# Attention outputs of two segments computed in the P @ V bank at the end of each unit, with six tiles of P

## The chip, the cores and the metric

The kernel runs on one core of one Trainium2 chip. The metric is the device time of one execution in microseconds (us). Before the change it is 1969.72 us, the median of 3 runs (1968.72 to 1974.34).

## The reference, cut to what matters

Two attentions over the same x (2048 rows, 512 columns, 32 heads of 16) are mixed by a gate per row. Side A is plain softmax attention over all 2048 keys. Side B works in four segments of 512 rows: causal attention inside the segment, plus a read from a linear memory that the segments before have filled.

```python
scores = jnp.einsum("bhqd,bhkd->bhqk", q, k) * scale      # A: all keys; B: own segment, masked
p = _softmax(scores, axis=-1)
o = jnp.einsum("bhqk,bhkd->bhqd", p, v)
a = o.reshape(B, S, D) @ wo
# B, per segment s:
o = g * (pq @ M) / (pq @ z + 1e-6) + (1.0 - g) * a_dot     # M, z: memory of the segments before
b = o @ wo
g = _sigmoid((x * gate_w).sum(-1, keepdims=True))
return g * a + (1 - g) * b
```

## The kernel before, in words

**Projections (the first 350 us or so).** q, k and v of both sides, the memory of side B and the gate are computed and left in DRAM.

**Units and slots.** The rest is attention. A unit is (side, group of 4 heads, segment of 512 query rows). Units of A and B alternate: A with 64 slots, then B with 10, so 74 slots a pair, 592 slots a segment (8 pairs) and 2368 in all, over four segments. A slot (`score_part`, L610) is one 512-column score product on TensorE into one of 3 `st` banks of PSUM; ScalarE turns it into P by an exponential (L633, and L630 for the last two slots of a B unit). Four slots fill one tile `p` of the pool `pp`, which has 4 such tiles.

**Maxima.** The scores of a unit need its row maxima first. For a unit that comes 96 slots later (`LEAD`), each slot also issues one product into one of 4 `sm` banks (`max_part`, L203), which VectorE reduces to a maximum (L218, L239, L243). The four banks are used in turn; `free` is the list of them.

**P @ V.** Slots come in bursts of three (`BURST`). After each burst `some_values` takes pieces of 128 columns of P from a queue, at most 3 (`MOST`), or 4 when the queue is longer than 8. Neighbouring pieces of one tile `p` go out as one group of four matmuls, one a head, side by side in four column strips of the array (L666). They add up in one PSUM bank, `ops`, for the whole unit. At the end of a unit ScalarE copies `ops` to SBUF (`oraw`, L670), and it goes to DRAM as `od`.

**Scaling.** `octet` handles 8 heads (two units) of a side, and also the memory read M. It has four steps at given slots: `load` (sums and values from DRAM, on SyncE's queue), `factors` 10 slots later (VectorE, L707 to L711), `factor` at 17 (the factors come back from DRAM, spread out, as `inv`), `scale` at 28 (GpSimd, L719, L721). For A and B it starts 16 slots after the end of the second unit's slots; the M octets start 14 slots apart, early in a segment.

**Outputs.** The scaled values times `wo` give the output: for a block of 128 rows, 8 octets by 4 column parts are 32 pieces (`piece`, L731), 128 a segment. `block_fill` borrows one of the four `sm` banks for a block, and the loop issues one piece after a burst, in a list `fill` that starts 24 slots after the segment's last A unit. So the outputs of segment 0 are made in the slots of segment 1, and so on; those of segment 3 partly at its end and partly after the loop. A burst in which a transposed maximum (L193) is due has no piece.

The order on TensorE is written out by this loop; its sequence in a burst is three times score and maximum product, then P @ V, then one piece or one transposed maximum.

```python
if n % BURST == BURST - 1 or n >= nS:
    some_values(n, MOST + (len(queue) > 8) if n < nS else 8)
```

Of the kernel before, what the change touches and what calls it, by code (L numbers as in the profile page):

```python
# [10 lines left out]
F32 = mybir.dt.float32  # L11
# [8 lines left out]
D = 512  # L20
H = 32
DH = 16
CH = 512
NCH = S // CH
KT = D // 128
NG = 8
NO = 4
# [8 lines left out]
LEAD = 96  # L36
BURST = 3
MOST = 3
GAP = {"A": 3, "B": 5}
MASK_T = 8  # L40
LATE_T = 8
# [5 lines left out]
def gated_mix(ctx, tc, x, xT, wqkv, a_wo, b_wq, b_wk, b_wv, b_wo, beta, gate_w, out):  # L47
# [508 lines left out]
    for (s, c), t in gate.items():  # L556
        nc.gpsimd.dma_start(t, gd["AB".index(s), c * CH:(c + 1) * CH].rearrange("(q t) -> q t", q=16)
                            .unsqueeze(0).broadcast_to([8, 16, 32]))
    pp = ctx.enter_context(tc.tile_pool(name="pp", bufs=4, reuse_waits="tile"))
    dp = ctx.enter_context(tc.tile_pool(name="dp", bufs=3, reuse_waits="tile"))  # L560
    va = ctx.enter_context(tc.tile_pool(name="va", bufs=2, reuse_waits="tile"))
    ob = ctx.enter_context(tc.tile_pool(name="ob", bufs=2, reuse_waits="tile"))
# [27 lines left out]
        vt[u] = t  # L590

    pt_ = {}
    stored = set()

    queue = []

    def score_part(n):

        u, j = slots[n]
        side, g, c = u  # L600
        q = qt[u]

        if j % 4 == 0:
            pt_[u, j // 4] = pp.tile([128, 4, CH], F32, tag="p", name="p")
        p = pt_[u, j // 4]
        h = (0, 2, 1, 3)[j % 4]

        def score(ps, h, b, k, n0, q0):

            nc.tensor.matmul(ps[:, n0:n0 + CH - q0], rows(k[:, :, b * 128:(b + 1) * 128], h, 50),  # L610
                             rows(q[:, :, q0:], h, 50), start=True, stop=True)

        def diagonal(x):
            nc.gpsimd.affine_select(out=x, in_=x, pattern=[[0, 4], [1, 128]], base=0, channel_multiplier=-1,  # L614
                                    compare_op=ALU.is_ge, fill=0.0)

        ps = st_ps.tile([128, CH], F32, tag="st", name="st")
        if side == "A":
            score(ps, h, j // 4 % 4, kt_[u, j // 16], 0, 0)
        else:  # L620
            k = kt_[u, c]
            if j < 8:
                score(ps, h, j // 4, k, 0, 128 * (j // 4))
                if j >= 4:
                    score(ps, h, 3, k, 384, 384)
            else:
                for f in range(2):
                    score(ps, 2 * (j - 8) + f, 2, k, 256 * f, 256)
        if side == "B" and j >= 8:
            nc.scalar.activation(p[:, 2 * (j - 8):2 * (j - 8) + 2, 0:256], ps.rearrange("p (h t) -> p h t", h=2), AF.Exp,  # L630
                                 scale=SCALE)
        else:
            nc.scalar.activation(p[:, h], ps, AF.Exp, scale=SCALE)  # L633
        if j % 4 == 3 or j == SLOTS[side] - 1:
            if side == "B":
                diagonal(p[:, :, 0:128])
                if j == 7:
                    diagonal(p[:, :, 384:])
            queue.extend((n + GAP[side], u, i) for i in range(j // 4 * 4, j + 1))

# [4 lines left out]
    def some_values(n, most):  # L645

        while queue and most and queue[0][0] <= n:
            _, u, i = queue.pop(0)
            most -= 1
            side, g, c = u  # L650
            w = 1
            while (queue and most and queue[0][0] <= n and queue[0][1] == u and (i + w) // 4 == i // 4
                   and (side == "A" or PIECES[i + w][0] == PIECES[i][0])):
                queue.pop(0)
                most -= 1
                w += 1
            p = pt_[u, i // 4]
            if side == "A":
                c0 = q0 = 128 * (i % 4)
                v = vt[u][:, i // 16, i // 4 % 4]  # L660
            else:
                b, c0, q0 = PIECES[i]
                v = vt[u][:, b]
            done = i + w == SLOTS[side]
            for h in range(4):
                nc.tensor.matmul(ops[32 * h:32 * h + 17, q0:q0 + 128 * w], v[:, 17 * h:17 * h + 17], p[:, h, c0:c0 + 128 * w],  # L666
                                 start=(i == 0), stop=done, tile_position=(0, 32 * h))
            if done:
                raw = ob.tile([128, CH], F32, tag="o", name="oraw")
                nc.scalar.copy(raw, ops)  # L670
                nc.sync.dma_start(od[side, c][4 * g:4 * g + 4].rearrange("h r t -> (h r) t"), raw)
                stored.add(u)
                return


# [3 lines left out]
        return rows.unsqueeze(0).broadcast_to([DH, 8, CH])  # L679

    held = {}


    beside = {}
# [4 lines left out]
    def octet(side, o, c, t0, vector=False):  # L689

        hs = slice(8 * o, 8 * o + 8)
        sums, rows, eng = (dend[c][hs], rdM[c][hs], nc.gpsimd) if side == "M" else (od[side, c][hs, 16], rd[side, c][hs], nc.gpsimd)
        if vector:
            eng = nc.vector
        k = {}

        def load():
            assert side == "M" or {(side, 2 * o, c), (side, 2 * o + 1, c)} <= stored
            k["rec"] = fr.tile([128, 32], F32, tag="rec", name="rec", bufs=3)
            nc.sync.dma_start(k["rec"], sums.rearrange("h (q t) -> h q t", q=16))  # L700
            if (side, c) not in held:
                held[side, c] = fr.tile([128, NO, CH], F32, tag="v" + side, name="v" + side, bufs=1 if side == "M" else 2)
            k["v"] = held[side, c][:, o]
            nc.sync.dma_start(k["v"], numd[c][:, o] if side == "M" else od[side, c][hs, 0:16].rearrange("h r t -> r h t"))

        def factors():
            nc.vector.reciprocal(k["rec"], k["rec"])  # L707
            if side == "B":
                nc.vector.scalar_tensor_tensor(k["rec"], k["rec"], ogh[:, o:o + 1], gate["B", c], op0=ALU.mult, op1=ALU.mult)
            else:  # L710
                nc.vector.tensor_mul(k["rec"], k["rec"], gate["A" if side == "A" else "B", c])  # L711
            nc.sync.dma_start(rows.rearrange("h (q t) -> (h q) t", q=16), k["rec"])

        def factor():
            k["inv"] = fr.tile([128, CH], F32, tag="inv", name="inv", bufs=4)
            nc.sync.dma_start(k["inv"], heads(rows))

        def scale():
            eng.tensor_mul(k["v"], k["v"], k["inv"])  # L719
            if side == "B" and c:  # L720
                eng.tensor_add(k["v"], k["v"], held["M", c][:, o])  # L721
        for n, f in ((0, load), (10, factors), (17, factor), (28, scale)):
            if t0 is None:
                f()
            else:
                at(t0 + n, f)

    def piece(ps, side, o, c, b, j, start, stop):

        for t in range(4):  # L730
            nc.tensor.matmul(ps[32 * t:32 * t + 32, 128 * j:128 * j + 128],  # L731
                             held[side, c][:, o, 128 * b + 32 * t:128 * b + 32 * t + 32], wos[side][:, o, 128 * j:128 * j + 128],
                             start=start, stop=stop, tile_position=(0, 32 * t))

# [6 lines left out]
    def block_fill(n, octets, c, b, then):  # L741

        ks = [(side, o) for o in octets for side in "AB"]
        for i in range(4 * len(ks)):
# [7 lines left out]
                    free.append(lent[c, b])  # L752
            fill.append((n, f))

    def leave(c, b):
        def then(ps):
            t = fr.tile([128, D], F32, tag="res", name="res", bufs=2)
            nc.scalar.copy(t, ps)
            nc.sync.dma_start(out_rows(c, b), t)
        return then  # L760
# [12 lines left out]
    at(180, lambda: load_wo("B", b_wo))  # L773
    last = NCH - 1
    for c in range(NCH):
        for o in range(NO):
            if c:

                octet("M", o, c, seg_end["B", c - 1] + (60 if c > 1 else 0) + 14 * o)
            for side in "AB":  # L780
                if (side, o, c) != ("A", NO - 1, last):
                    octet(side, o, c, end[side, 2 * o + 1, c] + 16)
        if c < last:
            for b in range(4):
                block_fill(seg_end["A", c] + 24, range(NO), c, b, leave(c, b))
    for b in range(4):
# [19 lines left out]
    while n < nS or queue or beside or filled[0] < len(fill):  # L806
# [12 lines left out]
            max_part(m, bank)  # L819
        run_todo(m)  # L820
        if n % BURST == BURST - 1 or n >= nS:
            some_values(n, MOST + (len(queue) > 8) if n < nS else 8)

            if any(e[0] < m + 1 for e in late):
                run_late(st_ps, "st", m + 1)
            else:
                for _ in range(1 if m < nS else 2):
                    if filled[0] < len(fill) and fill[filled[0]][0] <= n:
                        fill[filled[0]][1]()
                        filled[0] += 1  # L830
        n += 1
    octet("A", NO - 1, last, None, vector=True)
    for b in range(4):
        for j in range(4):
            close(0, "A", NO - 1, b, j)
            fill.pop()[1]()
        t = fr.tile([128, D], F32, tag="res", name="res", bufs=2)
        nc.vector.tensor_add(t, banks[b], part[b])
        (nc.scalar if b % 2 else nc.sync).dma_start(out_rows(last, b), t)
# [35 lines left out]
```

## Time and profile before

The profiled execution took 1971.88 us; its span is 1969.8 us, at a mean granted TensorE clock of 0.992. All times within the span count from its start.

| | |
|---|---|
| Median of 3 runs | 1969.72 us |
| Profiled execution, its span | 1971.88 us, 1969.8 us |
| TensorE (PE) busy | 98% |
| VectorE (DVE) busy | 82% |
| ScalarE (ACT) busy | 74% |
| DMA, mean | 116 GB/s |

The exponentials number the slots: by their starts, segment 0 begins at 348.1 us, segment 1 at 727.3, segment 2 at 1131.7, segment 3 at 1534.9, and the last slot is at 1944.2. PE rows are matmuls, PEld rows the loads of their weights. A float32 matmul of the program stands in the trace as two MATMULs, so one group of P @ V is x8, and one piece of an output is x8.

### The profile page before, as it was taken

The numbers are of one execution on the slowest core, as the hardware profiler recorded it, in microseconds if no ns is written. First come the engines' busy times: TensorE is split into PE (matmuls) and PEld (weight loads), VectorE is DVE, ScalarE is ACT, GpSimd is POOL, SyncE is SP. The second block draws the span as 40 slices with busy tenths as digits, with TensorE's granted clock in tenths as the row PEclk, the third lists the DMA queues.
The fourth block names the chain that finished last, engine by engine and source line by source line (L and its number), as shares of the span: only waits on it lengthen the run. The fifth ranks groups of instructions, "written<-read, shape, count | busy, mean of one in ns | idle before, by whom it ended". The sixth has DMA issues, their size and how long they took to land.

```text
span 1969.8 us, 50626 instructions
## 1 busy us (share of the span) xinstructions
PE 1932.7 (98%) x20361; PEld 1116.5 (57%) x20361; DVE 1618.2 (82%) x2768; ACT 1466.3 (74%) x2851; POOL 282.1 (14%) x497
## 2 busy tenths in 40 slices
PE   7999999999999999999999999999999999999997
PEld 5888765544444445555554455555544555555555
DVE  3235687899999998998999999999999999899820
ACT  3234332888888887888888887888888888888884
POOL 3000000211111112111112111111121112111210
PEclk9999999899999999999999999999999999999999
DMA  6567645334343435233324344324243343342211
GB/s 201 201 230 249 208 147 163 102 105 127 94 108 89 113 91 142 82 98 87 102 87 107 90 110 123 106 82 110 83 111 89 100 133 106 89 111 83 76 44 40
DMA packets 122504, 227.57 MB, mean 116 GB/s; under 512 B 34936, under 2 KB 46744, under 8 KB 121760
## 3 DMA queue, kind: packets, MB, share of 16 engines
q1 hardware_dynamic: 120688, 223.24, 38.9%
q8 instruction: 161, 2.64, 0.6%
q0 software_dynamic: 1296, 0.59, 0.2%
q14 instruction: 71, 0.58, 0.1%
q10 hardware_dynamic: 288, 0.52, 0.1%
HBM read 155.52 MB, written 67.52 MB: 113 GB/s over the span
## 4 chain that ended last, share of the span: by engine, by line
PE 91%; DVE 3%; DMA 2%; ACT 2%; issue 1%; SPq 0%; DVEq 0%; ACTq 0%
PE ops L666 30%; PE st L610 26%; PE sm L203 16%; PE pr L310 12%; PE sm L731 5%; DVE pm L218 2%; ACT p L633 1%; PE num L467 1%; PE mps L498 1%; PE mt_ps L193 1%; DMA qdA<-q 0%; ACT dg L229 0%; DMA raw<-xT 0%; DMA qdB<-q 0%; PE tps L490 0%
## 5 line engine op out<-in xcount | busy, mean ns | idle before, releaser
L633 ACT ACTIVATE p<-st 128x512 f32<-128x512 f32 x2304 | 1222.2, 605 | 239.7 <-PE sm L203 171.1
L218 DVE TENSOR_REDUCE pm<-sm 128x1 f32<-128x512 f32 x2048 | 1291.5, 683 | 117.3 <-PE sm L203 87.0
L203 PE MATMUL sm<-kA,qA 48*128 48x512 f32 x2048 | 786.4, 456 | 1.2 <-DVE pm L218 0.8
L610 PE MATMUL st<-qA,kA 50*128 50x512 f32 x2048 | 701.7, 438 | 3.8 <-ACT p L633 3.6
L666 PE MATMUL ops<-p,vA 128*17 128x384 f32 (+1 forms) x8184 | 576.5, 384 | 0.0
L610 PEld LDWEIGHTS st<-qA,kA 50*128 50x128 f32 x2048 | 332.8, 186 | 273.4 <-ACT p L633 203.3
L203 PEld LDWEIGHTS sm<-kA,qA 48*128 48x128 f32 x2048 | 338.6, 184 | 62.4 <-DVE pm L218 41.6
L666 PEld LDWEIGHTS ops<-p,vA 128*17 128x17 f32 x8184 | 165.0, 96 | 172.0 <-issue 161.7
L203 PE MATMUL sm<-kB,qB 48*128 48x128 f32 (+2 forms) x896 | 173.4, 297 | 0.4 <-DVE pmB L239 0.4
L203 PEld LDWEIGHTS sm<-kB,qB 48*128 48x128 f32 x896 | 134.4, 189 | 14.0 <-DVE pm L218 6.8
L230 POOL TENSOR_SCALAR_AFFINE_SELECT dg<-dg 128x512 f32<-128x512 f32 x128 | 81.2, 637 | 338.7 <-ACT dg L229 338.7
L610 PE MATMUL st<-qB,kB 50*128 50x384 f32 (+3 forms) x512 | 119.9, 341 | 2.7 <-ACT p L633 2.3
L358 DVE TENSOR_TENSOR q<-pr,q 128x512 fp32r<-128x512 f32 x64 | 44.0, 687 | 89.3 <-ACT q L351 79.6
L351 ACT CAST q<-pr 128x512 fp32r<-128x512 f32 x64 | 37.4, 585 | 98.5 <-PE pr L310 66.2
L731 PEld LDWEIGHTS sm<-woA,vA 128*32 128x32 f32 x2048 | 66.5, 113 | 69.1 <-issue 43.3
L731 PE MATMUL sm<-woA,vA 128*32 128x128 f32 x2048 | 98.0, 279 | 6.5 <-DVE vA L719 6.5
L610 PEld LDWEIGHTS st<-qB,kB 50*128 50x128 f32 x512 | 72.3, 185 | 50.7 <-ACT p L633 33.1
L731 PEld LDWEIGHTS sm<-woB,vB 128*32 128x32 f32 x2048 | 64.7, 110 | 63.1 <-issue 45.3
L186 POOL CAST ms<-nm 128x16 fp32r<-128x16 f32 x64 | 12.6, 197 | 599.4 <-DVE nm L179 540.2
L731 PE MATMUL sm<-woB,vB 128*32 128x128 f32 x2048 | 96.4, 273 | 0.0
L614 POOL TENSOR_SCALAR_AFFINE_SELECT p<-p 128x512 f32<-128x512 f32 x128 | 79.0, 635 | 100.2 <-ACT p L633 97.3
L666 PE MATMUL ops<-p,vB 128*17 128x128 f32 (+3 forms) x1104 | 89.6, 417 | 2.9 <-issue 2.3
(124 smaller groups left out, 1542.8 us busy)
## 6 DMA issues: line engine op xcount, KB each, us to landing
kA<-kdA SPq DMA_DIRECT2D x256, 128.0 KB
vA<-vdA SPq DMA_DIRECT2D x32, 544.0 KB
kA<-kdA SPq DMA_DIRECT2D x256, 64.0 KB
qdA<-q SPq DMA_DIRECT2D x32, 256.0 KB
kdA<-q SPq DMA_DIRECT2D x32, 256.0 KB
qdB<-q SPq DMA_DIRECT2D x32, 256.0 KB
qA<-qdA SPq DMA_DIRECT2D x64, 128.0 KB
kdB<-q SPq DMA_DIRECT2D x32, 256.0 KB
```

The costliest lines, as they stand in the source:

```text
L193: nc.tensor.matmul(pt[:32, :128], ms.rearrange("p r a h s -> p (r a h s)").bitcast(F32), identf, start=True, stop=True)
L203: nc.tensor.matmul(ps[:, n0:n0 + n], rows(qt[u][:, :, s * 128:(s + 1) * 128], h, 48), rows(k[:, :, k0:k0 + n], h, 48), start=True, stop=True)
L218: nc.vector.tensor_reduce(pm[:, h, s, kc:kc + 1], ps, axis=AX.X, op=ALU.max)
L230: nc.gpsimd.affine_select(out=dg, in_=dg, pattern=[[0, 4], [-1, 128]], base=0, channel_multiplier=1, compare_op=ALU.is_ge, fill=MASKED)
L310: nc.tensor.matmul(ps, l(a, k), r(b, k), start=(n == 0), stop=(n == 11))
L351: nc.scalar.copy(q1, ps)
L358: nc.vector.tensor_sub(q2, ps, q1.bitcast(F32))
L610: nc.tensor.matmul(ps[:, n0:n0 + CH - q0], rows(k[:, :, b * 128:(b + 1) * 128], h, 50), rows(q[:, :, q0:], h, 50), start=True, stop=True)
L614: nc.gpsimd.affine_select(out=x, in_=x, pattern=[[0, 4], [1, 128]], base=0, channel_multiplier=-1, compare_op=ALU.is_ge, fill=0.0)
L633: nc.scalar.activation(p[:, h], ps, AF.Exp, scale=SCALE)
L666: nc.tensor.matmul(ops[32 * h:32 * h + 17, q0:q0 + 128 * w], v[:, 17 * h:17 * h + 17], p[:, h, c0:c0 + 128 * w], start=(i == 0), stop=done ...
L731: nc.tensor.matmul(ps[32 * t:32 * t + 32, 128 * j:128 * j + 128], held[side, c][:, o, 128 * b + 32 * t:128 * b + 32 * t + 32], wos[side][: ...
```

## The change

- **P @ V falls behind.** The pool of P has 6 tiles in place of 4, and `some_values` takes a fourth piece when more than 6 pieces wait, in place of 8.
- **Outputs of segments 0 and 1** no longer go through `block_fill`. When an A unit of segment 1 or 2 has been stored, 16 pieces of the segment before are put on a list `shared`: one block of 128 rows, half of its columns. While the list has entries, each burst issues 4 of them in place of P @ V, in the bank `ops`, so for four bursts. Then ScalarE copies the half block (128 x 256) out and it is stored; two halves make a block.
- **Outputs of segments 2 and 3** are made as before, with a borrowed `sm` bank.
- **Octets** start when their two units have been stored: 8 slots later for A and B; an M octet starts 4 slots after the even B unit of its pair. The M values have two tiles of one octet in place of one of four, and `inv` has 3 tiles in place of 4.

```diff
+NP = 6
+SHARED = (0, 1)
...
-    pp = ctx.enter_context(tc.tile_pool(name="pp", bufs=4, reuse_waits="tile"))
+    pp = ctx.enter_context(tc.tile_pool(name="pp", bufs=NP, reuse_waits="tile"))
...
                 stored.add(u)
+                if side == "B" and c and g % 2 == 0:
+                    octet("M", g // 2, c, n + 4)
+                if (side, g ^ 1, c) in stored and u != ("A", NG - 1, NCH - 1):
+                    octet(side, g // 2, c, n + 8)
+                if side == "A" and c - 1 in SHARED:
+                    shared.extend(half_block(c - 1, g // 2, g % 2))
...
-            k["inv"] = fr.tile([128, CH], F32, tag="inv", name="inv", bufs=4)
+            k["inv"] = fr.tile([128, CH], F32, tag="inv", name="inv", bufs=3)
...
+    shared = []
+
+    def half_block(c, b, half):
+
+        ps = ops[:, 0:256]
+        ks = [(side, o) for o in range(NO) for side in "AB"]
+        for i in range(16):
+            def f(i=i):
+                piece(ps, *ks[i // 2], c, b, 2 * half + i % 2, i == 0, i == 15)
+                if i == 15:
+                    t = fr.tile([128, D], F32, tag="res", name="res", bufs=2)
+                    nc.scalar.copy(t[:, 0:256], ps)
+                    nc.sync.dma_start(out_rows(c, b)[:, 256 * half:256 * half + 256], t[:, 0:256])
+            yield f
...
-        for o in range(NO):
-            if c:
-
-                octet("M", o, c, seg_end["B", c - 1] + (60 if c > 1 else 0) + 14 * o)
-            for side in "AB":
-                if (side, o, c) != ("A", NO - 1, last):
-                    octet(side, o, c, end[side, 2 * o + 1, c] + 16)
-        if c < last:
+        if c < last and c not in SHARED:
             for b in range(4):
                 block_fill(seg_end["A", c] + 24, range(NO), c, b, leave(c, b))
...
         if n % BURST == BURST - 1 or n >= nS:
-            some_values(n, MOST + (len(queue) > 8) if n < nS else 8)
+            if shared:
+                for _ in range(4):
+                    shared.pop(0)()
+            else:
+                some_values(n, MOST + (len(queue) > 6) if n < nS else 8)
```

More of the change, by code (lines that the diff above doesn't have):

```diff
@@ L592, in gated_mix @@
     pt_ = {}
+    order_p = {}
     stored = set()
@@ L604, in score_part @@
             pt_[u, j // 4] = pp.tile([128, 4, CH], F32, tag="p", name="p")
+            order_p[u, j // 4] = len(order_p)
+            assert not queue or order_p[queue[0][1], queue[0][2] // 4] > len(order_p) - 1 - NP
         p = pt_[u, j // 4]
@@ L681, in gated_mix @@
     held = {}
+    scaled = set()
     beside = {}
@@ L700, in load @@
             nc.sync.dma_start(k["rec"], sums.rearrange("h (q t) -> h q t", q=16))
-            if (side, c) not in held:
-                held[side, c] = fr.tile([128, NO, CH], F32, tag="v" + side, name="v" + side, bufs=1 if side == "M" else 2)
-            k["v"] = held[side, c][:, o]
+            if side == "M":
+                k["v"] = held["M", c, o] = fr.tile([128, CH], F32, tag="vM", name="vM", bufs=2)
+            else:
+                if (side, c) not in held:
+                    held[side, c] = fr.tile([128, NO, CH], F32, tag="v" + side, name="v" + side, bufs=2)
+                k["v"] = held[side, c][:, o]
             nc.sync.dma_start(k["v"], numd[c][:, o] if side == "M" else od[side, c][hs, 0:16].rearrange("h r t -> r h t"))
@@ L720, in scale @@
             if side == "B" and c:
-                eng.tensor_add(k["v"], k["v"], held["M", c][:, o])
+                eng.tensor_add(k["v"], k["v"], held.pop(("M", c, o)))
+            scaled.add((side, o, c))
         for n, f in ((0, load), (10, factors), (17, factor), (28, scale)):
@@ L728, in piece @@
     def piece(ps, side, o, c, b, j, start, stop):
+        assert (side, o, c) in scaled
         for t in range(4):
-            nc.tensor.matmul(ps[32 * t:32 * t + 32, 128 * j:128 * j + 128],
+            nc.tensor.matmul(ps[32 * t:32 * t + 32, 128 * (j % (ps.shape[1] // 128)):128 * (j % (ps.shape[1] // 128)) + 128],
                              held[side, c][:, o, 128 * b + 32 * t:128 * b + 32 * t + 32], wos[side][:, o, 128 * j:128 * j + 128],
@@ L821, in gated_mix @@
         if n % BURST == BURST - 1 or n >= nS:
-            some_values(n, MOST + (len(queue) > 8) if n < nS else 8)
+            if shared:
+                for _ in range(4):
+                    shared.pop(0)()
+            else:
+                some_values(n, MOST + (len(queue) > 6) if n < nS else 8)
             if any(e[0] < m + 1 for e in late):
@@ L832, in gated_mix @@
     octet("A", NO - 1, last, None, vector=True)
+    assert len(stored) == len(units)
     for b in range(4):
```

## The prediction

> **What bounds the kernel now.** I read the busy shares first, then the stages, then the waits of two stages, then single bursts.
>
> The page's first part, and what the chain of waits says by line:
>
> ```profile
> span 1969.8 us, 50626 instructions
> ...
> PE 1932.7 (98%) x20361; PEld 1116.5 (57%) x20361; DVE 1618.2 (82%) x2768; ACT 1466.3 (74%) x2851; POOL 282.1 (14%) x497
> ...
> PE ops L666 30%; PE st L610 26%; PE sm L203 16%; PE pr L310 12%; PE sm L731 5%; DVE pm L218 2%; ACT p L633 1%; PE num L467 1%; PE mps L498 1%; PE mt_ps L193 1%; DMA qdA<-q 0%; ACT dg L229 0%; DMA raw<-xT 0%; DMA qdB<-q 0%; PE tps L490 0%
> ```
>
> TensorE looks like the bound, and nearly all of the chain lies on it. By stages it is less simple. Columns: stretch, us, then busy us of PE, PEld, DVE, ACT, POOL. The first three rows are six pairs of units without output pieces (segment 0), five pairs with them, and two stretches that are the whole of segments 1 and 2; the row after them is of L731 alone in the five pairs.
>
> ```profile
> 445.50:727.30 281.80, 278.43 (x2802) 137.88 (x2800) 273.44 (x469) 249.06 (x493) 42.36 (x79) 1.00 0.37 102
> ...
> 780.70:1037.50 256.80, 255.70 (x3210) 144.94 (x3208) 232.92 (x388) 211.35 (x415) 36.79 (x67) 1.00 0.33 93
> ```
>
> ```profile
> 727.30:1131.70 404.40, 402.10 (x4760) 220.11 (x4758) 372.75 (x633) 336.02 (x662) 65.94 (x112) 1.00 0.37 100
> 1131.70:1534.90 403.20, 400.82 (x4766) 219.79 (x4764) 373.09 (x633) 336.73 (x661) 66.81 (x112) 1.00 0.36 101
> ```
>
> ```profile
> 780.70:1037.50 256.80, 44.16 (x880) 28.39 (x880) 1.00 0.33 93
> ```
>
> A pair without pieces takes 281.8 / 6 = 47.0 us, or 1.90 us for each of its 24.67 bursts; there DVE is busy 273.44 / 281.8 = 97%. A pair with pieces takes 256.8 / 5 = 51.4 us, with 880 / 8 / 5 = 22 pieces, and DVE falls to 91%. So PE's busy share of 99% in both does not tell who waits; the waits do. Columns: us in total, times, longest. First 445.50 to 727.30, then 780.70 to 1037.50:
>
> ```profile
> PEld st L610 <- ACT p L633: 78.5, 175, 0.7
> ```
>
> ```profile
> PEld st L610 <- ACT p L633: 19.7, 88, 0.6
> ...
> DVE pm L218 <- PE sm L203: 16.2, 43, 1.0
> ```
>
> Without pieces PE waits for the banks that ScalarE and VectorE empty; with pieces VectorE waits for PE. Segments 1 and 2 pass from the one to the other: pieces in some 5 of 8 pairs, none in the rest.
>
> **The price of each kind of work on PE.** Rows are start and length; the difference between starts is what a step costs. In order: two pieces of P (after them a score), four pieces in two groups, a piece of an output behind four pieces in two groups, behind four in one group, and two pieces of an output.
>
> ```profile
> 560.00 0.63 PE L666 MATMUL ops<-p,vA 128*17 128x256 f32 x8
> 560.55 0.50 PE L610 MATMUL st<-qA,kA 50*128 50x512 f32 x1
> ...
> 561.80 0.52 PE L666 MATMUL ops<-p,vA 128*17 128x384 f32 x4
> ```
>
> ```profile
> 447.06 1.06 PE L666 MATMUL ops<-p,vB 128*17 128x384 f32 x16
> 448.05 0.49 PE L610 MATMUL st<-qA,kA 50*128 50x512 f32 x1
> ...
> 448.94 0.41 PE L666 MATMUL ops<-p,vB 128*17 128x256 f32 x4
> ```
>
> ```profile
> 719.61 1.06 PE L666 MATMUL ops<-p,vA 128*17 128x128 f32 x16
> 720.60 0.50 PE L610 MATMUL st<-qB,kB 50*128 50x512 f32 x1
> ...
> 721.58 0.30 PE L666 MATMUL ops<-p,vA 128*17 128x128 f32 x4
> ```
>
> ```profile
> 1004.85 1.06 PE L666 MATMUL ops<-p,vA 128*17 128x128 f32 x16
> 1005.73 0.40 PE L731 MATMUL sm<-woB,vB 128*32 128x128 f32 x8
> 1006.06 0.50 PE L610 MATMUL st<-qA,kA 50*128 50x512 f32 x1
> ```
>
> ```profile
> 831.09 1.05 PE L666 MATMUL ops<-p,vB 128*17 128x512 f32 x8
> 831.96 0.40 PE L731 MATMUL sm<-woA,vA 128*32 128x128 f32 x8
> ```
>
> ```profile
> 1896.14 0.62 PE L731 MATMUL sm<-woB,vB 128*32 128x128 f32 x16
> 1896.69 0.50 PE L610 MATMUL st<-qB,kB 50*128 50x512 f32 x2
> ```
>
> - Two pieces of P and the return to the scores: 0.55 us. Four: 0.99. So a piece is 0.22 and the return some 0.12.
> - An output piece and the return: 0.33; two: 0.55. So a piece of either kind costs 0.22, and the return is paid once a burst.
> - Four pieces of P in two groups: 0.88; in one group: 0.87. **Merging groups saves 0.01 us**, not a matmul's time.
> - Three exponentials in a row take 1.57 us and three maxima 1.88 (below).
> - Scores and maxima after four pieces: 0.89 (first) and 0.98 (last of the 40 such bursts of the first stretch); their mean is 0.96. After two pieces, 1.25: the short rest of the burst is given back, as ScalarE and VectorE are not done.
>
> ```profile
> 563.10 1.57 ACT L633 ACTIVATE p<-st 128x512 f32<-128x512 f32 x3 [0.43 <-PE sm L203]
> ...
> 564.22 1.88 DVE L218 TENSOR_REDUCE pm<-sm 128x1 f32<-128x512 f32 x3
> ```
>
> **The change, part by part.**
>
> *Merged groups.* In the order in which the two programs issue, groups of P @ V fall from 1161 to 742. 419 times 0.01 us is about 4 us over the kernel, within the sums below. The Trainium skill, "TensorE: Matmul & The Clock Gate", Part 1, gives a fixed cost of about 2.5 ns to each matmul; with 8 matmuls of the trace to a group that would be an estimated 8 us, and the rows show half of it.
>
> *Outputs moved.* The pieces of segments 0 and 1 stay 256, at 0.22 each wherever they stand: moving them saves no time of PE. What changes is the company they keep. In the changed order, segment 1 has 197 bursts: 127 with four pieces of P, 30 with four output pieces, 40 with one to three pieces of P. No bank is lent, so maxima have four. The sum for the segment:
> - 127 x (0.99 + 0.95) = 246. I take 0.95 and not 0.96, because in a row of long bursts ScalarE and VectorE have more time than in the 40 measured ones, which stand among short ones. Bounds: 0.89 and 1.05.
> - 30 x (0.33 + 3 x 0.22 + 1.15) = 64. These bursts fall on the slots of the B unit, whose scores come in several products. Such a burst is no cheaper than the one at 488.55 below, 1.16, and no dearer than that at 583.63, 1.50; I take the lower, as those after it have four pieces of rest.
> - 40 x 1.90 = 76, a short burst lasting what the stretch without pieces gives per burst.
> - 11 transposed maxima beside four pieces at some 0.2 us: 2 (two matmuls and a change; a guess between 0.1 and 0.3).
>
> ```profile
> 488.55 0.44 PE L610 MATMUL st<-qB,kB 50*128 50x384 f32 x1
> ...
> 489.71 0.30 PE L666 MATMUL ops<-p,vA 128*17 128x128 f32 x4
> ```
>
> ```profile
> 583.63 0.44 PE L610 MATMUL st<-qB,kB 50*128 50x384 f32 x1
> ...
> 585.13 0.52 PE L666 MATMUL ops<-p,vB 128*17 128x384 f32 x4 [0.47 <-issue]
> ```
>
> Together 388 us. From VectorE's side: its 372.75 us of work at the 97% that it reaches when it is the bound make 384. I take 387 for each of segments 1 and 2: 404.4 - 387 = 17.4 and 403.2 - 387 = 16.2, **33.6 us saved**. Ends: 373 (VectorE without a gap) and 404 (nothing gained).
>
> *Uneven P @ V in segments 0 and 3.* There the pieces of P per burst go from 3, 4, 3, 2 to 3, 1, 4, 4. In segment 0 VectorE is the bound at 97% and has a backlog of up to four banks at 0.63 us each, more than the 0.99 us of four pieces: nothing lost, 0. In segment 3 a bank is lent and an output piece stands in each burst, so two bursts in a row are long and starve VectorE, and the one-piece burst cannot give it all back: 0.08 us for each of some 49 cycles, **4 us lost**. Bounds for both: -3 and +21 (below).
>
> *The bank `ops`, handed over twice a unit.* A wait is added: P @ V of the next unit stands behind ScalarE's copy of the half block, and behind it on PE all scores. Before, P @ V waited 1.2 us in all for 64 such copies (the copy's view; "who waited for it"):
>
> ```profile
> L670 ACT COPY oraw<-ops x64: 586/608/632, 397.8 to 1946.6; 128x512 f32<-128x512 f32 x64
> ...
>   PEld ops L666: 1.2, 6
> ```
>
> A burst's scores and maxima lie between the hand-overs as before, and the new copy is half as wide. I take 0. Upper end: three exponentials ahead of the copy (1.57 us) and the copy at 0.6, less 0.95 of scores, 1.2 us; 32 hand-overs make 38 us. The Trainium skill, "PSUM — Partial Sum Buffer", section "PSUM bank collisions raise a hardware error", asks that two engines be kept apart by whole bank and quadrant; it speaks against putting a second user into this bank, since the unused half does not help, and the row above is what the trace shows of the price so far.
>
> *The rest at nothing.* Loads of octets move to 8 slots (some 5 us) after the store. The store and the load that waits for it on SyncE's queue took 1.99 and 2.06 us at the end of the kernel; k tiles queued behind are asked for 20 slots ahead. Without that cover, SyncE would hold them 2 to 4 us a unit. VectorE's factors keep their 10 slots after the load. Eight more stores, four full copies less and 16 half copies more change ScalarE's 83% by under 1%.
>
> ```profile
> 1947.19 1.99 DMA odA<-oraw
> ...
> 1949.19 2.06 DMA rec<-odA
> ```
>
> More tiles of P remove no wait that the rows show.
>
> **Sum.** 1971.88 (the profiled execution: span 1969.8 and 2.1 around it) - 33.6 + 4 = 1942.3. The median of the runs lies 2.2 lower, so 1940.
>
> **The rivals.**
> - *VectorE becomes the only bound in segments 1 and 2.* With four banks and long bursts it never starves: 375 us a segment, 57.6 saved, nothing lost in segment 3: 1912. For it: it reaches 97% today. Against: B-unit bursts stretch PE to 1.15 and more, and no backlog covers four in a row.
> - *Nothing is gained.* PE's work is unchanged but for 4 us; if the scores keep their present mean length behind any rest, segments 1 and 2 lose only that: 1966 to 1970. For it: PE shows 99% in every stage. Against: 0.96 after four pieces, 1.25 after two.
> - *Slower: uneven bursts.* A burst with one piece gives nothing back if its scores last 1.6 us or more (they wait for VectorE's banks and for exponentials), while the four-piece bursts still cost 1.95. A cycle of four then costs 0.2 us more; 98 cycles in segments 0 and 3 make 21 lost. The same starving at the end of the catch-up runs (scores 1.05, 0.1 more in each of 127 bursts) leaves segments 1 and 2 only 7 us: +7 on balance, 1977. For it: 1.25 already after two pieces. Against: VectorE at 97% in segment 0 cannot be held up by PE alone.
> - *Hand-overs at their upper end*: 38 us back, 1978; counted with the one before.
>
> **How the numbers follow.** A difference of 0.3% (6 us) is about what a measurement of this kernel can tell from none. Chances: forecast (1925 to 1955) 0.54; VectorE the only bound 0.18; a small gain, 1955 to 1964, 0.06; nothing gained 0.10; slower 0.12. Faster 0.78, same 0.10, slower 0.12. For eight in ten the range takes in the VectorE rival from 1914 up and most of the case of no gain: 1914 to 1968.
>
> **What would show it.** Right: segments 1 and 2 at 380 to 394 us with DVE at 95 to 98%, scores waiting for ScalarE less in them, groups x8 of 512 columns at 0.87 up to the next step, segment 0 within 3 us of before, segment 3 a few us longer. Wrong: P @ V or output pieces waiting for copies of `ops` for more than 5 us in all; VectorE waiting for PE over 20 us in a segment; a kA load that PE waits for.

## The result, and the profile after

The changed kernel takes 1940.28 us (median of 4 runs, 1939.61 to 1941.45), against 1969.82 us before (median of 4 runs, 1968.72 to 1974.34). The ratio is 0.9846, with a 95% interval of 0.9829 to 0.9863: faster by 29.5 us, where 29.7 were forecast.

The page of the changed kernel, first part and chain by line (L671 is P @ V, L615 the scores, L205 the products for the maxima, L748 the output pieces):

```profile
span 1938.8 us, 44063 instructions
...
PE 1897.4 (98%) x17009; PEld 993.5 (51%) x17009; DVE 1611.9 (83%) x2768; ACT 1467.0 (76%) x2859; POOL 281.7 (15%) x497
...
PE ops L671 30%; PE st L615 27%; PE sm L205 14%; PE pr L312 11%; PE ops L748 3%; PE sm L748 2%; ACT p L638 2%; DVE pm L220 1%; DMA qdA<-q 1%; PE num L469 1%; DMA kdB<-q 1%; PE mt_ps L195 1%; ACT dg L231 1%; PE mps L500 0%; DMA qdB<-q 0%
```

TensorE has 3352 MATMULs less in the trace and is as busy as before, 98%. The gain must be looked for by stages: stretch, us, then busy us of PE, PEld, DVE, ACT, POOL. The rows are six pairs of segment 0, the whole of segments 1 and 2, and the first seven pairs of segment 3.

```profile
444.10:728.10 284.00, 279.21 (x2240) 122.02 (x2240) 273.66 (x469) 248.52 (x493) 42.38 (x79) 0.99 0.37 101
728.10:1110.80 382.70, 380.49 (x3758) 177.88 (x3762) 368.71 (x633) 336.22 (x665) 65.50 (x112) 1.00 0.41 105
1110.80:1494.20 383.40, 380.67 (x3839) 178.35 (x3828) 369.55 (x634) 337.36 (x666) 67.06 (x114) 1.00 0.41 106
1494.20:1862.80 368.60, 365.29 (x3909) 188.81 (x3909) 316.27 (x534) 297.75 (x583) 60.14 (x102) 1.00 0.35 94
```

Segments 1 and 2 fell from 404.4 and 403.2 to 382.7 and 383.4, and VectorE works 96% of segment 1 in place of 92%. Segment 0 is 2 us longer, and segment 3 longer by far more than the forecast: to the last slot 419.7 us, against 409.3.

The waits between TensorE and VectorE in segment 1, before and after. Columns: us in total, times, longest.

```profile
PEld st L610 <- ACT p L633: 50.5, 162, 0.7
...
DVE pm L218 <- PE sm L203: 21.3, 53, 1.2
...
PEld sm L203 <- DVE pm L218: 11.8, 45, 0.6
```

```profile
PEld st L615 <- ACT p L638: 117.2, 184, 0.9
...
DVE pm L220 <- PE sm L205: 9.1, 20, 1.0
...
PEld sm L205 <- DVE pm L220: 1.1, 6, 0.2
```

Two waits shrank: VectorE's for a product, and TensorE's for a free `sm` bank (the weight load of a maximum product that waits for a reduction). The second, 11.8 us, has almost gone. The wait of score weights for ScalarE grew from 50.5 to 117.2 us, and the segment is shorter all the same: the total of this wait does not say how much time is lost by it.

### The profile page after: what moved, and what is told of

Its sections match the earlier page's. It is cut to its first block, busy times and chain, and to the rows that moved or that the text cites. A ratio compares the mean times of both kernels' runs of the same rounds, so it can differ in the third digit from the quotient of the medians.

```text
span 1938.8 us, 44063 instructions
## 1 busy us (share of the span) xinstructions
PE 1897.4 (98%) x17009; PEld 993.5 (51%) x17009; DVE 1611.9 (83%) x2768; ACT 1467.0 (76%) x2859; POOL 281.7 (15%) x497
## 4 chain that ended last, share of the span: by engine, by line
PE 89%; DMA 3%; ACT 3%; DVE 3%; issue 1%; POOL 0%; SPq 0%; ACTq 0%; POOLq 0%; DVEq 0%
PE ops L671 30%; PE st L615 27%; PE sm L205 14%; PE pr L312 11%; PE ops L748 3%; PE sm L748 2%; ACT p L638 2%; DVE pm L220 1%; DMA qdA<-q 1%; PE num L469 1%; DMA kdB<-q 1%; PE mt_ps L195 1%; ACT dg L231 1%; PE mps L500 0%; DMA qdB<-q 0%
## 5 line engine op out<-in xcount | busy, mean ns | idle before, releaser
L205 PE MATMUL sm<-kA,qA 48*128 48x512 f32 x2048 | 757.7, 450 | 1.3 <-DVE pm L220 1.3
L615 PE MATMUL st<-qA,kA 50*128 50x512 f32 x2048 | 702.9, 439 | 7.8 <-ACT p L638 7.1
L671 PE MATMUL ops<-p,vA 128*17 128x512 f32 (+2 forms) x4912 | 561.2, 529 | 0.0
L615 PEld LDWEIGHTS st<-qA,kA 50*128 50x128 f32 x2048 | 336.1, 186 | 412.6 <-ACT p L638 336.9
L205 PEld LDWEIGHTS sm<-kA,qA 48*128 48x128 f32 x2048 | 338.3, 185 | 37.7 <-DVE pm L220 22.9
L205 PE MATMUL sm<-kB,qB 48*128 48x128 f32 (+2 forms) x896 | 171.5, 295 | 0.6 <-DVE pmB L241 0.5
L671 PEld LDWEIGHTS ops<-p,vA 128*17 128x17 f32 x4912 | 81.7, 95 | 165.0 <-issue 153.9
L205 PEld LDWEIGHTS sm<-kB,qB 48*128 48x128 f32 x896 | 135.0, 188 | 10.6 <-DVE pm L220 2.6
L615 PE MATMUL st<-qB,kB 50*128 50x384 f32 (+3 forms) x512 | 120.9, 342 | 3.3 <-ACT p L638 2.4
L615 PEld LDWEIGHTS st<-qB,kB 50*128 50x128 f32 x512 | 72.6, 186 | 66.3 <-ACT p L638 52.0
L671 PE MATMUL ops<-p,vB 128*17 128x512 f32 (+3 forms) x1024 | 89.2, 444 | 1.7 <-issue 1.5
L241 DVE TENSOR_REDUCE pmB<-sm 128x4 f32<-128x512 f32 x128 | 87.1, 681 | 1.2 <-PE sm L205 1.2
L235 DVE TENSOR_REDUCE pmB<-dg 128x4 f32<-128x512 f32 x128 | 86.7, 677 | 0.8 <-POOL dg L232 0.8
L231 ACT COPY dg<-sm 128x512 f32<-128x512 f32 x128 | 76.4, 597 | 1.8 <-DVE pmB L235 1.8
L722 DVE RECIPROCAL rec<-rec 128x32 f32<-128x32 f32 x44 | 15.1, 343 | 71.2 <-DMA rec<-odA 40.3
```

The source lines that it names most:

```text
L205: nc.tensor.matmul(ps[:, n0:n0 + n], rows(qt[u][:, :, s * 128:(s + 1) * 128], h, 48), rows(k[:, :, k0:k0 + n], h, 48), start=True, stop=True)
L231: nc.scalar.copy(dg, blocked(ps))
L235: todo.append((m + MASK_T, lambda: nc.vector.tensor_reduce(to, dg.rearrange("p (h s) t -> p h s t", h=2), axis=AX.X, op=ALU.max)))
L241: nc.vector.tensor_reduce(pm[:, 1, h, 3:7], blocked(ps), axis=AX.X, op=ALU.max)
```

## The experiments

All segment times below are from the starts of the exponentials in one profiled execution of each kernel; medians are of 4 runs. A pair is an A and a B unit, 74 slots, eight to a segment. Segment 3 counts to the last slot.

| kernel | median | ratio (95%) | seg. 0 | seg. 1 | seg. 2 | seg. 3 |
|---|---|---|---|---|---|---|
| before | 1969.82 | | 379.2 | 404.4 | 403.2 | 409.3 |
| changed | 1940.28 | 0.9846 (0.9829 to 0.9863) | 381.4 | 382.7 | 383.4 | 419.7 |
| e1_no_shared | 1994.81 | 1.0124 (1.0107 to 1.0141) | 383.0 | 408.5 | 411.1 | 417.4 |
| e2_spread | 1983.09 | 1.0062 (1.0047 to 1.0077) | 379.6 | 409.7 | 408.9 | 410.9 |
| e3_three_banks | 1990.29 | 1.0094 (1.0079 to 1.0109) | 383.8 | 406.0 | 407.3 | 421.9 |
| e4_threshold | 1935.12 | 0.9813 (0.9796 to 0.9830) | 380.1 | 382.8 | 383.3 | 411.7 |
| e5_shared3 | 1919.68 | 0.9732 (0.9707 to 0.9757) | 385.3 | 382.7 | 383.3 | 396.5 |
| e6_both | 1917.90 | 0.9720 (0.9700 to 0.9740) | 382.9 | 382.7 | 383.3 | 396.5 |
| e7_bank_seg0 | 1990.75 | 1.0096 (1.0065 to 1.0127) | 400.2 | 404.7 | 403.3 | 409.2 |
| e8_four_banks | 1945.84 | 0.9854 (0.9825 to 0.9884) | 379.3 | 390.9 | 389.5 | 410.9 |
| e9_four_banks_spread | 1942.11 | 0.9852 (0.9838 to 0.9867) | 382.8 | 389.4 | 389.0 | 408.1 |
| e10_no_part | 1911.12 | 0.9697 (0.9681 to 0.9714) | 380.9 | 382.8 | 383.4 | 388.9 |

Segment 0's first pair alone varies from 50 to 55 us: it took 51.1 us before and 54.7 in e9_four_banks_spread, whose segment 0 is the same work. So 4 us in segment 0 mean little.

My theory at first was that of the prediction: segments 1 and 2 gain because output pieces are moved out of short stretches and into long bursts, in which scores and maxima do not wait; segments 0 and 3 lose by the uneven 3, 1, 4, 4. The rivals were the fourth `sm` bank, which is no longer lent, and the fewer groups of P @ V.

**No outputs at unit ends.**

```diff
-SHARED = (0, 1)
+SHARED = ()
```

> The changed kernel with all outputs made piece by piece in borrowed sm banks again; six tiles of P, the earlier fourth piece and the earlier octets stay. My theory: the merged groups are worth about 4 us of TensorE and the uneven 3, 1, 4, 4 costs more than that; what segment 3 lost in the changed kernel (10.4 us) is lost in segments 1 and 2 as well, so 1998 to 2008 us, slower than before. Rival, that fewer matmul groups and more tiles of P make the gain: 1940 to 1966 us. If the earlier octets cost or gain something, segment 1's first pair (53.4 us before, 47.8 after) shows it.

1994.8 us. The merged groups and six tiles of P make no gain; with the lent bank and without the output pieces at unit ends, segments 1 to 3 lose 4 to 8 us each. The first pair of segment 1 took 52.2 us, 1.2 less than before, and that of segment 2 took 53.2, 2.8 more: the earlier octets show no gain. The theory holds here in kind, 3 us below its range.

**The pieces spread out, in a lent bank.**

```diff
-                for _ in range(1 if m < nS else 2):
+                for _ in range(0 if 592 <= n < 1776 and n // BURST % 4 == 3 else 1 if m < nS else 2):
```

> The kernel before, with the output pieces of segments 0 and 1 left out of every fourth burst and so spread over the whole of the next segment (17 a pair in place of 22), still one a burst in a borrowed sm bank, P @ V as before. My theory, that gain comes from spreading the pieces over stretches where TensorE waits and from putting them into long bursts: the first half alone, segments 1 and 2 at 392 to 400 us, 1946 to 1962 us in all. Rival, that the gain is the fourth sm bank: nothing, 1966 to 1973 us.

Neither: 1983.1 us, slower than before. The bank is now lent through the whole of segments 1 and 2, and both are longer, 409.7 and 408.9. In segment 1 the seven later pairs hold 912 / 8 / 7 = 16 pieces each and take 357.1 / 7 = 51.0 us, hardly less than the pairs of before with 22 (51.4). The piece rows of those seven pairs:

```profile
779.60:1136.70 357.10, 45.76 (x912) 29.44 (x912) 1.00 0.32 92
```

Spreading pieces saves nothing if the bank stays away for longer. My theory fell here.

**The changed kernel with three banks.**

```diff
+        if n == 592:
+            kept = free.pop(0)
+        if n == 1776:
+            free.append(kept)
```

> The changed kernel with one sm bank laid aside during segments 1 and 2, so that maxima have three as when a block borrows one. My theory: 2 to 6 us more in each of the two segments, 1944 to 1952 us. Rival, that the gain is the fourth bank: both segments back at about 404 us, 1976 to 1984 us.

1990.3 us, above both ranges. My theory's 2 to 6 us a segment are far off. Segments 1 and 2 are back at 406 and 407 us, 2 to 4 us over the rival's 404, and segments 0 and 3 stay as long as in the changed kernel: without the fourth bank, everything else that the change does in segments 1 and 2 is worth nothing. The waits of this run in segment 1:

```profile
PEld sm L205 <- DVE pm L220: 17.2, 47, 0.7
DVE pm L220 <- PE sm L205: 16.4, 47, 1.0
```

TensorE's wait for a bank is 17.2 us, where the changed kernel has 1.1 and the kernel before 11.8; VectorE's wait for a product is 16.4, where they have 9.1 and 21.3. I read it so: three banks hold the products of one burst, so TensorE waits when VectorE is behind, and VectorE runs dry when TensorE then does four pieces of P.

**A lent bank without pieces.** The new theory needed the bank by itself. In the kernel before, segment 0 has no pieces; there a bank was laid aside.

```diff
+        if n == 0:
+            kept = free.pop(0)
+        if n == 592:
+            free.append(kept)
```

> The kernel before, with one sm bank laid aside during the slots of segment 0, where no output piece is issued; nothing else. New theory, after the spread pieces and the three banks: the lent bank itself makes a pair of units last 51 us, whether 16, 17 or 22 pieces are in it, so segment 0 goes from 379 to some 400 to 412 us without a single piece, 1990 to 2004 us in all. Rival, my first account, that a piece costs its 0.22 us of TensorE and the stretch with pieces is long for that: segment 0 longer by 0 to 6 us, 1970 to 1976 us.

Segment 0 takes 400.2 us in place of 379.2, without one instruction more in the program. Six pairs, with their waits:

```profile
451.40:747.70 296.30, 294.92 (x2801) 150.27 (x2800) 277.96 (x469) 251.18 (x493) 42.52 (x79) 1.00 0.35 97
```

```profile
PEld sm L203 <- DVE pm L218: 15.6, 56, 0.7
DVE pm L218 <- PE sm L203: 9.1, 23, 1.0
```

A pair goes from 47.0 to 49.4 us, 2.4 us for the bank alone, and the wait for a free bank rises from 4.2 to 15.6 us (the row of before is below). That is less than the 51 that I expected: the bank is not all of it.

```profile
DVE pm L218 <- PE sm L203: 6.1, 14, 1.0
...
PEld sm L203 <- DVE pm L218: 4.2, 19, 0.4
```

**Pieces without a lent bank.** The reverse: the kernel before, its pieces at their places, but added into `ops`.

```diff
...
+                if c < 2:
+                    piece(ops, *ks[i // 4], c, b, i % 4, None, None)
+                    if i == 4 * len(ks) - 1:
+                        then(wos["A"][:, 0])
+                    return
...
```

> The kernel before, with the pieces of segments 0 and 1 added into the bank of P @ V, at 17 columns of weights in place of 32, one a burst while a unit's sum is open, so that no sm bank is lent in segments 1 and 2; the copies of those blocks read SBUF. It leaves out the outputs of the first two segments and spoils the values of P @ V; the number and the places of the instructions are those of before. New theory (the lent bank): segments 1 and 2 at 380 to 392 us, 1924 to 1948 us in all. Rival, my first account (the pieces' own time in short stretches): both segments stay at 400 to 405 us, 1963 to 1973 us.

Segments 1 and 2 take 390.9 and 389.5 us: two thirds of the change's gain in them (13.5 of 21.7 us in segment 1) by leaving the bank where it is. The pieces do not stay quite at their places: they wait for an open sum, so a pair holds up to 20 in place of 23 and they reach one pair further. A later pair takes 49.0 us, with 768 / 8 / 5 = 19 pieces (five pairs; the second row is of the pieces alone):

```profile
777.20:1022.10 244.90, 242.56 (x3098) 130.51 (x3096) 230.34 (x388) 210.24 (x413) 36.70 (x67) 1.00 0.34 96
```

```profile
777.20:1022.10 244.90, 38.55 (x768) 22.57 (x768) 1.00 0.34 96
```

So 47.0 without either, 49.4 with the bank lent, 49.0 with 19 pieces, 51.4 with the bank lent and 22 pieces, 51.0 with the bank lent and 16: **a pair costs 2.4 us for the bank and 0.1 us for each piece, and the two add up** (47.0 + 2.4 + 22 x 0.1 = 51.6; with 16, 51.0). A piece takes 0.22 us of TensorE, so about half of that seems to go into time that TensorE spent waiting anyway. For a segment that is 12.8 us for its 128 pieces wherever they stand, and 2.4 us for each pair in which the bank is away: 5 to 6 pairs before, nearly 8 in the run with the pieces spread, which is why that was slower.

**The same, spread out.** What makes the other 8 us a segment?

```diff
-                for _ in range(1 if m < nS else 2):
+                for _ in range(0 if 592 <= n < 1776 and n // BURST % 4 == 3 else 1 if m < nS else 2):
```

> The run with the pieces in the bank of P @ V one a burst, and these left out of every fourth burst, so that they spread over the whole segment (17 a pair); outputs left out and spoiled as there. It asks what makes the 8 us a segment by which the changed kernel is shorter than that run (382.7 against 390.9). If spreading does it: 383 to 386 us in segments 1 and 2, some 1932 to 1938 us in all. If the bursts of four pieces and the P @ V that catches up do it: 389 to 393 us, 1942 to 1948 us.

389.4 and 389.0 us: with four banks too, spreading is worth 0.5 to 1.5 us a segment, as it must be if a piece costs the same everywhere. The last 6 to 7 us come with the changed kernel's bursts: four output pieces or four pieces of P at a time.

The starts of TensorE's rows tell more. They split segment 1 into the time of P @ V and output pieces, up to the next score, and the time of scores and maxima, up to the next piece. The last column is how much the second time exceeds 0.95 us a burst, first behind bursts with fewer than four pieces of either kind, then behind the others; in brackets, how many such bursts there are.

| segment 1 of | pieces, us | scores and maxima, us | over 0.95 us a burst: short bursts, others |
|---|---|---|---|
| before | 183.4 | 220.2 | 22.4 (80), 10.6 (117) |
| e8_four_banks | 183.4 | 206.8 | 18.1 (82), 1.6 (115) |
| e9_four_banks_spread | 180.5 | 208.1 | 18.6 (69), 2.3 (128) |
| changed | 180.8 | 199.7 | 12.7 (40), 0.8 (156) |
| e3_three_banks | 180.4 | 223.2 | 17.9 (40), 19.1 (156) |

The pieces take TensorE as long as before (in the last three rows, 12 or 13 output pieces fall into the next segment, 2.6 to 2.9 us). So the gain lies in scores and maxima. Keeping the bank takes away nearly all of the excess behind long bursts; of what remains, the changed kernel saves 5 to 6 us because it has 40 short bursts in place of 69 to 82. With three banks the same order of bursts has as much excess as the kernel before.

**The threshold of before in segments 0 and 3.**

```diff
-                some_values(n, MOST + (len(queue) > 6) if n < nS else 8)
+                some_values(n, MOST + (len(queue) > (6 if 592 <= n < 1776 else 8)) if n < nS else 8)
```

> The changed kernel with the fourth piece of P taken from 7 waiting on in segments 1 and 2 alone, and from 9 on, as before the change, in segments 0 and 3. My theory, that the 3, 1, 4, 4 of segments 0 and 3 costs what they lost: segment 3 back from 419.7 to about 409 us and segment 0 by 2, 1926 to 1931 us. Rival, that segment 3 is longer for the moved octets or the six tiles: 1938 to 1942 us.

Segment 3 returns from 419.7 to 411.7 us, segment 0 from 381.4 to 380.1. The profiled run, 1929.3 us, is the fastest of its four; the other three took 1935 to 1936. The median is so 4 us above the expectation and 3 below the rival's range; by stages of the profiled execution the expectation holds, within 3 us. There 3, 1, 4, 4 costs 8 of the 10 us that segment 3 lost; what is left lies near the kernels whose segment 3 is that of before (408.1 to 410.9). The medians differ by only 5.2 us, so the 8 us of this one execution may be too much.

**Outputs of segment 2 at unit ends as well**, and then also the threshold of before in segment 0.

```diff
-SHARED = (0, 1)
+SHARED = (0, 1, 2)
...
-            if shared:
+            if shared and n < nS:
...
     octet("A", NO - 1, last, None, vector=True)
+    while shared:
+        shared.pop(0)()
```

> The changed kernel with the outputs of segment 2 made at unit ends too, in segment 3; the last half block is issued after the last octet's loads. Both the lent bank and the uneven 3, 1, 4, 4 then leave most of segment 3: its first 518 slots go from 368.7 to 336 to 342 us, 1905 to 1918 us in all. If the loss in segment 3 is due to something else (the octets, six tiles), 1930 us or more.

> As the run before this one, and the fourth piece of P from 9 waiting on in segment 0, as before the change: 1 to 3 us less than that run, 1903 to 1916 us.

1919.7 and 1917.9 us. Five pairs of segment 3 fall to 47.4 to 48.2 us, as in segments 1 and 2; the last three stay at 52.5, 53.8 and 50.8. In the first two of these a bank is lent for the first octets of segment 3's own outputs, which are issued there besides the shared pieces; in the last, two closing pieces go out after each burst. Both runs end some 2 us above their ranges, by those three pairs; the threshold in segment 0 is below what these runs can tell.

**No bank lent at all.** The pieces of those octets join the closing ones, which use all four banks when the maxima are done.

```diff
-    for b in range(4):
-        block_fill(nS - 208, range(1), last, b, keep(b))
...
-    closing = [(side, o) for o in range(1, NO) for side in "BA"]
+    closing = [(side, o) for o in range(NO) for side in "BA"]
...
-        nc.vector.tensor_add(t, banks[b], part[b])
+        nc.vector.tensor_copy(t, banks[b])
```

> The run with outputs of three segments at unit ends and the earlier threshold in segment 0; besides, no bank is lent near the end of segment 3 for the first octets of its outputs: those 32 pieces go to the closing ones, which already use all four banks once the maxima are done. Theory of the lent bank: pairs 30 to 32, now 52.5, 53.8 and 50.9 us, go to 48 to 50 each; the 32 pieces at 0.22 us (7 us) fall partly in the 11 us in which TensorE waits for the last octet: 1906 to 1914 us. Rival, that the pieces and not the bank stretch those pairs: 1914 to 1922 us.

1911.1 us, ratio 0.9697 (0.9681 to 0.9714): the fastest version, 29 us under the changed kernel. The first seven pairs of segment 3, in the run before this one and here:

```profile
1495.00:1840.70 345.70, 343.33 (x3641) 166.86 (x3643) 312.36 (x534) 297.46 (x587) 59.85 (x101) 1.00 0.37 99
```

```profile
1493.60:1831.70 338.10, 335.50 (x3381) 157.06 (x3381) 311.10 (x534) 295.27 (x582) 59.96 (x101) 1.00 0.37 101
```

The time is within the expected range, the pairs only in part: 30 and 31 go to 47.7 and 51.1 us, and 32 stays at 50.8, as its 59 pieces are the same in both runs. The run does not separate the bank from the pieces, since pair 30 also goes from 37 to 19 pieces and pair 31 from 37 to 22. By the prices above, bank and pieces together should save 4.2 and 3.8 us; they saved 4.8 and 2.7.

## Why the prediction was right, and which steps of it were not

**The time was right, and so was its main sum.** Segments 1 and 2 at 387 us each came to 382.7 and 383.4. By terms:
- Four pieces of P and what follows: 0.99 + 0.95 forecast, 246 us and 2 for the transposed maxima. The 127 such bursts of segment 1 come to 248, with 0.95 behind them on average. One of them (0.99, then 0.90):

```profile
834.28 1.05 PE L671 MATMUL ops<-p,vA 128*17 128x512 f32 x8
835.27 0.50 PE L615 MATMUL st<-qA,kA 50*128 50x512 f32 x1
...
836.17 1.05 PE L671 MATMUL ops<-p,vA 128*17 128x512 f32 x8
```

- Four output pieces: 0.99 + 1.15 forecast. They cost 1.01, and what follows 0.90 here. Over such bursts of segment 1 the second part is 0.96 on average. The step that failed is "These bursts fall on the slots of the B unit": only 8 of the 29 that lie whole in the segment are followed by B scores, and even with these it is 0.90 to 1.01 us, so the two bursts of segment 0 that the 1.15 came from were no measure of them. This term, 64 us, was 5 too high, which is about what the segment came out lower.

```profile
824.64 0.65 PE L748 MATMUL ops<-woA,vA 128*32 128x128 f32 x16
825.10 0.62 PE L748 MATMUL ops<-woB,vB 128*32 128x128 f32 x16
825.65 0.50 PE L615 MATMUL st<-qA,kA 50*128 50x512 f32 x1
...
826.55 0.42 PE L748 MATMUL ops<-woA,vA 128*32 128x128 f32 x7
```

- The 40 short bursts: 76 forecast, 75 measured.

**The reason given was wrong in its first step.** The prediction read the two stretches of before as "without pieces" and "with pieces", and said that moving pieces changes "the company they keep". The stretches differ in two things, and the other one, the lent bank, weighs as much: 2.4 us a pair, against 2.0 to 2.2 for its pieces. A piece costs the time of the kernel 0.1 us there, not the 0.22 that it takes on TensorE. The sum came out right because its prices (0.95 after four pieces, 1.90 for a short burst, VectorE's 97%) were taken from the stretch with four banks, which is what the changed segments have. That these were the right ones was luck as far as the reason goes; as prices they were read from rows, and held. "No bank is lent, so maxima have four" stood there as a remark and was the main cause; three banks in the changed kernel undo its whole gain in the two segments. The company counts too, but only for the last 6 to 7 us a segment, by the smaller number of short bursts.

**The signs it named are mixed.** Segments 1 and 2, VectorE's 96%, groups of 512 columns at 0.87 and segment 0 came as said. But "scores waiting for ScalarE less in them" failed: 117.2 us in segment 1 where 50.5 were. Of its marks of being wrong, VectorE waits for TensorE 28.9 us in segment 3, over the 20; in segments 1 and 2 it waits 9.1 and 8.7. No matmul waits for a load of kA.

**Merged groups** at nothing much: right, and shown by the run without outputs at unit ends. The price of 0.01 us came from rows rounded to 0.01: before an output piece, four pieces of P take 0.875 us in two groups and 0.870 in one, averaged over 98 and 73 places. That is 0.005 us a group, about 2 us over the kernel in place of 4.

**Uneven P @ V** was right in kind and too small: 4 us forecast for segment 3, 10.4 measured, of which the threshold returns 8. The size that failed is "the one-piece burst cannot give it all back: 0.08 us for each of some 49 cycles"; 8 us over 49 cycles are 0.16, though that 8 is of one execution. The bound of 21 for both segments held. In segment 0 with four banks the forecast of 0 is within the spread.

**The bank `ops` handed over** was put at 0 and the mark for "wrong" at 5 us of waiting. All waits for its copies, whole kernel:

```profile
  PEld ops L671: 4.7, 18
  PEld ops L748: 3.4, 5
  PE ops L748: 2.3, 5
```

That is 10.4 us where 1.2 were before, 2.3 of it waits of a matmul and the rest of weight loads; none was for the 16 new half copies. (In a segment these are eight in place of four full ones; the prediction counted the full ones of one segment and the halves of two.) So the mark was passed. What it costs in time was not tried by itself; segments 1 and 2 came out below the forecast with it.

**The rivals.** Of VectorE as the only bound, half came true: VectorE reaches 96% in segments 1 and 2, and these lie between the forecast's 387 and that rival's 375 us, nearer to the forecast; segment 3 does not follow, and a bank is still lent there. The case of no gain is what three banks give in the two segments. The slower case did not come. Its own sum does not close either: 98 cycles at 0.2 us are 20 and not 21, and 0.1 us in each of 127 bursts leaves 8 us of the 33.6 in both segments, so its time would be near 1982 and not 1977. The run without outputs at unit ends shows how large such a loss can be, 23 us over the time before, where the uneven bursts meet a lent bank in three segments.

## What to carry to other kernels

A PSUM bank that is borrowed from a rotating set can cost for as long as it is away, whatever the work done in it: here one of four cost 2.4 us in 47, with or without that work, so side work is better placed in a bank whose own work can stand aside for it. Where a stretch with extra work is slower, look at what else differs in that stretch before giving the difference to the work; laying the resource aside where there is no such work, and doing the work without it, separates the two in two runs. And taking work four at a time helped here where VectorE had four banks to live on meanwhile, and hurt where it had three.

## What the runs showed of the hardware

- Output pieces and pieces of P, both in column strips of the array, follow each other at 0.22 us each with nothing between them (four pieces of P before an output piece take 0.88, before a score 0.99); the return to the scores, which use the array in row halves, costs 0.11 to 0.12 us. The Trainium skill, "TensorEngine Tiling (Array Packing)", section "Tiling Modes", says that a change of tiling mode drains TensorE, and gives no time. The 0.12 us on the way back agrees with that, but no run here separates the drain from the rest of the step, and no row prices the way from scores to pieces.
- TensorE's busy share was 99% at 47.0 us a pair (278.43 of 281.80 us, segment 0 before) and at 52.7 (365.29 of 368.60, segment 3 after): in this kernel it does not tell the stages apart. In segment 1 the wait of weight loads for an `sm` bank did (11.8 us before, 1.1 in the changed kernel, 17.2 with three banks), and so did VectorE's share (92%, then 96%).
